# Summing the first and the last two chunks of a second product tile by tile, where two token tiles take over the accumulation banks of two others

## The chip, the cores and the metric

The kernel runs on one core of one Trainium2 chip. That core has TensorE (PE, the matrix unit), VectorE (DVE), ScalarE (ACT), GpSimd (POOL) and SyncE (SP, which here only starts transfers). Each engine works through its own queue of instructions in order; semaphores tie the queues together. The metric is the time of one execution of the whole program in device microseconds (us), as a median over runs. Matrix products leave their results in eight PSUM banks of 128 partitions by 512 fp32 values.

## What the kernel must compute

The reference is an attention layer with a decay, followed by a feed-forward layer over the same tokens (B = 8 batches, H = 8 heads, S = 576 positions, 64 values per head: 4608 tokens of 512 values; w_in is 512 x 2048, w_out 2048 x 512):

```python
scores = scale * q @ k^T
decay  = cum[:, None] - cum[None, :]        # cum = cumsum(log(clip(f)))
scores = where(causal, -1e9, scores + decay)
attn   = softmax(scores) @ v                # per batch and head
x      = attn, as 4608 tokens x 512
h      = x @ w_in                           # first product, 4608 x 2048
g      = max(h, 0) + log1p(exp(-abs(h)))
out    = g @ w_out                          # second product, 4608 x 512
```

All of it is fp32. The kernel reaches that accuracy on PE by splitting each operand in a high and a low part and adding three products of parts: high x high, high x low and low x high.

## The kernel before, in words

**Blocks, chunks, tiles.** The feed-forward part goes through the tokens in ten blocks: two of 256 tokens, then eight of 512. The 2048 columns of `h` are cut into 16 chunks of 128. For one wide block (512 tokens) the first product fills one bank `h` per chunk (`up_part`, L989, 12 matmuls at L1023), ACT and DVE turn it into `g` and its parts `gh` and `gl` (`gate`, L1050), and the second product adds chunk after chunk into the accumulators: a block has four output tiles of 128 tokens, each needs one bank (`acc_0` to `acc_3`), and every chunk adds three matmuls of 512 columns into each (`products`, L1103, the matmul at L1108: `gh` with the high part of w_out, `gh` with its low part, `gl` with its high part).

**Two passes and the switch.** The banks are shared with attention: four have the tag `att`, two `h`, and only two `acc`. So blocks 2 to 7 sum two tiles at a time (`ahead = 2`). In the first pass `down_part` (L1117) adds each chunk into `acc_0` and `acc_1` as the chunks are made, and `keep` (L1080) stores the half of `gh` and `gl` that belongs to tiles 2 and 3 to DRAM (`g_d`). After chunk 15 `finish` (L1185) copies each accumulator to a buffer `ob` (the copy is recorded at L209, on ACT or DVE) and stores it to `out` (L1195). The second pass, `second` (L1152), loads the stored parts back, two chunks in a load (`gh_0b`, `gl_0b` hold chunks 0 and 1, up to `gh_7b`), and adds them into `acc_2` and `acc_3`, which take the same two banks. This place, where the last chunks go into `acc_0` and `acc_1` and the first into `acc_2` and `acc_3`, is called a switch below; there are six, one for each of blocks 2 to 7. The last two blocks get two banks from attention, which is over by then, and have no switch.

**Order.** Nothing of the order is written out by hand. Every piece of work is added to a list with what it needs and which banks or buffers it takes (`tags`); a planner (`Plan`, L46) gives each engine its queue by list scheduling: of the next 700 pieces it takes again and again the one that by its table of costs can start first, the earlier added one where two tie. Feed-forward pieces are added between those of attention by a budget of time (`run_ffn`). `add_block` (L1229) lines up a block's pieces: the second product of a chunk runs `LAG` = 2 chunks behind its first product, and the last six pieces of a block's second pass are held back and put between the first chunks of the next block, where no second product is at hand yet.

**Attention** runs through the same queues: q and k come as `raw` (L653), are split and moved into `T` (L209, a cast on ACT or DVE, and L692), scores `s` (L736, L737), their row minima `negm` (L741, DVE), the weights `p` (L761, an exponential on ACT), the row sums (L773, L774), `p` times the reciprocal `rsum` (L783 on ACT, L785 on POOL), the transposes of `p` into `b` (L815), their parts `ph` (L209) and `pl` (L830), the product with v, `o` (L863, L869), and the shift of `o` into the rows `x` of the feed-forward part (L887 on ACT, L896 on DVE). Transposed names such as `s_1` count the rows' tiles in one head.

Of the kernel before, what the change touches and what calls it, by code (L numbers as in the profile page):

```python
# [212 lines left out]
def tile_decay_attention_softplus_ffn(  # L213
# [19 lines left out]
    NT, DM = out.shape  # L233
# [706 lines left out]
    def ffn_block(i):  # L940
# [175 lines left out]

        def down_part(u, k):  # L1117
            box, ready, kept = st["g", u]
            fc = u * nk + k
            tags = (("acc", "acc") + late_banks)[:ahead]  # L1120

            def mm(e):
                if fc == 0:
                    begin(range(ahead), tags)
                if plain:
                    for tt in range(ntile):
                        e.matmul(  # L1127
                            st["acc", tt], box["g"][:, (2 * k + tt) * P : (2 * k + tt + 1) * P],
                            w_out32[fc], start=fc == 0, stop=fc == NFC - 1,
                        )  # L1130
                    return
                products(e, fc, range(ahead), *(box[x][:, k * nt :] for x in "hl"))

            op = add(
                on_pe32(DM * ahead) if plain else on_pe(DM, 3 * ahead), mm,
                after=ready + ([w_out_ready[fc]] if plain else w_out_done[fc]) + st["downs"][-1:],
                takes=tags if fc == 0 else (),
            )
            st["downs"].append(op)
            if plain:  # L1140
                w_out_read[fc] = [op]
                splits_left.extend([lambda: split_w_in(fc), lambda: split_w_out(fc)])
            if k == nk - 1:
                give("gh", [op])
                if not plain:
                    give("gl", [op] + kept)
                if kept:

                    plan.gives[op][-2][1][0] += 1
                    plan.gives.setdefault(kept[0], []).append(plan.gives[op][-2])  # L1150

        def second(fp, k):  # L1152

# [10 lines left out]
            def mm(e):  # L1164
                if fc == 0:
                    begin(range(ahead, ntile), ("acc",) * 2)
                products(
                    e, fc, range(ahead, ntile), *(st[x, fp][:, k * TB :] for x in ("gh", "gl"))
                )

            if k == 0:
                need = [st["kept", fc], st["kept", fc + 1]]
# [3 lines left out]
            op = add(  # L1176
                on_pe(DM, 3 * (ntile - ahead)), mm, after=[st["second", fp]] + st["downs"][-1:],
                takes=("acc",) * 2 if fc == 0 else (),
            )
            st["downs"].append(op)  # L1180
            if k:
                give("gh", [op])
# [25 lines left out]
        for u in range(NFC // nk):  # L1208
# [6 lines left out]
            downs.append([(down_t, lambda u=u, k=k: down_part(u, k)) for k in range(nk)])  # L1215
        downs[-1].append((0.0, lambda: finish(range(ahead))))
        tail = []
        if ahead < ntile:
            tail = [
                (down_t, lambda fp=fp, k=k: second(fp, k)) for fp in range(NFP) for k in range(2)  # L1220
            ] + [(0.0, lambda: finish(range(ahead, ntile)))]
        return [(0.0, split_x)], ups, downs, tail
# [6 lines left out]
    def add_block(i):  # L1229
        head, ups, downs, tail = ffn_block(i)  # L1230

        n = min(6, kept_units[0], len(ffn)) if ffn and not late else 0
        last = [ffn.pop() for _ in range(n)][::-1]
        ffn.extend(head)
        for u, d in zip(ups, downs):
            ffn.extend(u)
            late.append(d)
            if last:
                ffn.extend(last[:2] if len(late) <= LAG else last)
                last = last[2:] if len(late) <= LAG else []  # L1240
            if len(late) > LAG:
# [149 lines left out]
```

## Time and profile before

| what | value |
|---|---|
| median of three runs | 1230.14 us (1228.51, 1230.14, 1230.23) |
| the profiled execution | 1233.55 us, of which its span is 1231.4 us and 2.15 us lie around it |
| PE busy | 1209.8 us of the span (98%) in 6512 matmuls |
| DVE, ACT, POOL busy | 868.2 us (70%), 863.5 us (70%), 140.4 us (11%) |
| granted clock of PE | mean 0.993 of full speed |
| transfers | 168.40 MB, a mean of 137 GB/s over the span |
| matmuls of the two-pass second product (L1108) | 3 x 352 as the page groups them, some 0.39 to 0.41 us each from start to modelled end |
| first matmul of acc_2 at the six switches | at 368.10, 498.37, 629.10, 762.94, 896.81 and 1027.38 us of the span |

Matmuls overlap, so that the time from one start to the next is what a matmul costs, not its own duration. A row of the timeline gives start, duration, engine, line, operation, output and inputs; what stands in brackets at its end is the time that the engine had waited for the piece named there. Rows of ACT and DVE overlap slightly too, by an instruction's tail.

### The profile page before, as it was taken

The page shows a single profiled execution, that of the slowest core. Times are in us where ns is not written, and L with a number is a line of the kernel's source. Part 1 is how long each engine was busy: PE and PEld are TensorE (multiplying, and loading weights), DVE is VectorE, ACT ScalarE, POOL GpSimd, SP SyncE. Part 2 cuts the span into 40 slices and gives each one's busy share as a digit, 9 for nine tenths or more (in the row PEclk, how much of TensorE's full clock was granted, in tenths as well). Part 3 has the DMA queues.
Part 4 walks back from the last instruction along what each step waited for, and adds up shares of the span by engine and source line. Part 5 has one row for each costly group of instructions (what it writes and reads, how often), then busy time and mean ns, then how long its engine had stood idle before and what let it go on. Part 6 is the DMA issues. An engine that isn't in the chain of part 4 may idle for free.

```text
span 1231.4 us, 19804 instructions
## 1 busy us (share of the span) xinstructions
PE 1209.8 (98%) x6512; PEld 1007.8 (82%) x6512; DVE 868.2 (70%) x2138; ACT 863.5 (70%) x2055; POOL 140.4 (11%) x121
## 2 busy tenths in 40 slices
PE   7899999999999999999999999999999999999998
PEld 5676688888888888888888888888888888888887
DVE  6988889998787778767786778577866774223322
ACT  4576688888787777777787787687867874444543
POOL 3621012011011000010001000100011000000000
PEclk9799999999999999999999999999999999999999
DMA  7865435335455454654474446453565435211210
GB/s 214 259 179 146 133 93 152 112 91 177 121 173 174 130 151 138 186 168 120 122 220 133 138 126 186 129 165 108 149 174 169 122 95 160 80 52 52 86 52 35
DMA packets 100199, 168.40 MB, mean 137 GB/s; under 512 B 10496, under 2 KB 74008, under 8 KB 100096
## 3 DMA queue, kind: packets, MB, share of 16 engines
q1 hardware_dynamic: 100096, 167.13, 46.0%
q8 instruction: 52, 0.85, 0.3%
q14 instruction: 51, 0.42, 0.1%
HBM read 127.85 MB, written 39.24 MB: 136 GB/s over the span
## 4 chain that ended last, share of the span: by engine, by line
PE 82%; DVE 7%; ACT 5%; DMA 3%; issue 2%; POOL 1%; SPq 0%; DVEq 0%; POOLq 0%; ACTq 0%
PE h L1023 28%; PE acc L1108 27%; PE b L815 7%; PE o L869 6%; PE s L737 3%; PE s L736 3%; DMA raw<-in_qkT 2%; PE h L1004 2%; PE s L734 2%; ACT p L761 2%; PE fill L1299 2%; PE o L863 1%; PE acc L1127 1%; DVE s L741 1%; ACT p L783 1%
## 5 line engine op out<-in xcount | busy, mean ns | idle before, releaser
L1023 PE MATMUL h<-xh,wih 128*128 128x512 f32 (+1 forms) x576 | 230.5, 403 | 0.6 <-DVE gl L1078 0.6
L761 ACT ACTIVATE p<-s,negm 128x288 f32<-128x288 f32 (+7 forms) x384 | 183.1, 480 | 51.7 <-DVE negm L741 49.1
L1023 PE MATMUL h<-xl,wih 128*128 128x512 f32 (+1 forms) x576 | 216.8, 379 | 0.0
L1070 DVE SCALAR_TENSOR_TENSOR h<-h,e 128x512 f32<-128x512 f32 x136 | 95.1, 699 | 136.8 <-ACT e L1062 135.0
L741 DVE CUSTOM_DVE_ANT_0 s<-s,cmask 128x288 f32<-128x288 f32 (+5 forms) x320 | 137.4, 437 | 63.1 <-PE s L737 53.4
L785 POOL TENSOR_SCALAR p<-p,rsum 128x448 f32<-128x448 f32 (+3 forms) x72 | 91.3, 1273 | 788.5 <-DVE rsum L774 436.9
L1056 ACT ACTIVATE e<-h 128x512 f32<-128x512 f32 x144 | 85.7, 595 | 117.5 <-PE h L1023 115.9
L830 DVE TENSOR_TENSOR pl<-b,ph 128x512 fp32r<-128x512 f32 (+1 forms) x224 | 126.1, 569 | 49.3 <-ACT ph L209 48.2
L1023 PE MATMUL h<-xh,wl 128*128 128x512 f32 (+1 forms) x576 | 148.6, 380 | 0.0
L815 PE MATMUL b<-ident,p 128*128 128x128 f32 x960 | 145.7, 275 | 1.1 <-POOL p L785 0.3
L1108 PE MATMUL acc<-woh_dt_float32r,gh 128*128 128x512 f32 x352 | 143.4, 407 | 0.0
L1108 PE MATMUL acc<-woh_dt_float32r,gl 128*128 128x512 f32 x352 | 137.8, 392 | 0.0
L1108 PE MATMUL acc<-wol_dt_float32r,gh 128*128 128x512 f32 x352 | 137.2, 390 | 0.0
L815 PEld LDWEIGHTS b<-ident,p 128*128 128x128 f32 x960 | 114.1, 140 | 24.0 <-issue 3.2
L1023 PEld LDWEIGHTS h<-xh,wih 128*128 128x128 f32 x576 | 108.8, 189 | 16.9 <-DVE gl L1078 0.8
L1023 PEld LDWEIGHTS h<-xh,wl 128*128 128x128 f32 x576 | 104.8, 188 | 21.4
L1023 PEld LDWEIGHTS h<-xl,wih 128*128 128x128 f32 x576 | 108.8, 189 | 14.4
L783 ACT ACTIVATE p<-p,rsum 128x192 f32<-128x192 f32 (+6 forms) x227 | 106.7, 536 | 18.2 <-DVE rsum L774 17.5
L209 ACT CAST ph<-b 128x512 fp32r<-128x512 f32 (+1 forms) x150 | 81.7, 546 | 52.2 <-PE b L815 50.9
L1078 DVE TENSOR_TENSOR gl<-h,gh 128x512 fp32r<-128x512 f32 x136 | 93.5, 687 | 27.5 <-ACT gh L209 26.2
L869 PE MATMUL o<-ph,vhl 128*128 128x320 f32 x448 | 105.2, 264 | 0.0
L736 PE MATMUL s<-T 128*64 128x64 f32 x336 | 99.6, 306 | 4.0 <-ACT p L761 2.9
(156 smaller groups left out, 2382.0 us busy)
## 6 DMA issues: line engine op xcount, KB each, us to landing
wl<-wil_d SPq DMA_DIRECT2D x72, 512.0 KB
raw<-in_qkT SPq DMA_DIRECT2D x112, 288.0 KB
g_d<-gh SPq DMA_DIRECT2D x96, 128.0 KB
g_d<-gl SPq DMA_DIRECT2D x96, 128.0 KB
vr<-in_vR SPq DMA_DIRECT2D x64, 160.0 KB
out<-ob SPq DMA_DIRECT2D x36, 256.0 KB
sto<-in_w_out SPq DMA_DIRECT2D x11, 512.0 KB
sti<-in_w_in SPq DMA_DIRECT2D x9, 512.0 KB
```

The source lines that it names most:

```text
L736: e.matmul(o, qA[:, q0:end], kA[:, a:z], start=True, stop=False)
L741: e.tensor_tensor_reduce(out=box["o"], in0=box["o"], in1=cmask[0:n_q, right - w : right], scale=-0.125, scalar=m0 if i else 3.0e38, op0=AL ...
L761: e.activation(o, box["o"], AF.Exp, bias=m1, scale=-1.0, accum_out=acc)
L783: e.activation(a, a, AF.Copy, scale=f_)
L785: e.tensor_scalar(a, a, f_, None, ALU.mult)
L815: e.transpose(box["ps"][:, at : at + P], pt[pi][:, c : c + P], ident)
L830: e.tensor_sub(box["l"], box["ps"][:, pad : pad + w], box["h"].bitcast(F32))
L869: e.matmul(box["ps"][:, a - g0 : z - g0], st["vhl"][:, vc, :], pbox[x][:, o : o + z - a], start=i == 0 and m == 0, stop=i == len(todo) - 1 ...
L1023: e.matmul(o, l, r, start=m == 0, stop=m == 11)
L1070: e.scalar_tensor_tensor(h, h, 0.0, box["e"], ALU.max, ALU.add)
L1078: e.tensor_sub(box["l"], box["t"], box["h"].bitcast(F32))
L1108: e.matmul(st["acc", tt], l, r[fc], start=fc == 0 and m == 0, stop=fc == NFC - 1 and m == 2,)
```

## The change

The second product's pieces can now hold one tile instead of two. `down_part` and `second` take a list of tiles. In blocks 2 to 7 the last two chunks of the first pass (14 and 15) are no longer added chunk by chunk into both accumulators: `acc_0` gets chunk 14 and chunk 15, is finished (copied and stored), and only then `acc_1` gets its chunks 14 and 15 and is finished. In the second pass the first load (chunks 0 and 1) and the last (chunks 14 and 15) are treated in the same way: both chunks into `acc_2`, then both into `acc_3`, with a `finish` after each tile in the last. A bank is asked for tile by tile too: `acc_2` takes one bank, `acc_3` the other when its first piece comes. The buffers `gh` and `gl` of chunk 14 are given back only after the last tile's piece, and `gh` and `gl` of chunk 15 likewise. `add_block` holds back nine pieces of the second pass instead of six; the last pieces are now half as long, and two, three and the rest of them go between the next block's chunks.

```diff
--- before.py
+++ after.py
@@ -1114,14 +1114,14 @@
             for tt, tag in zip(tiles, tags):
                 st["acc", tt] = bank(tag, f"acc{i}_{tt}")
 
-        def down_part(u, k):
+        def down_part(u, k, tiles=range(ahead)):
             box, ready, kept = st["g", u]
             fc = u * nk + k
-            tags = (("acc", "acc") + late_banks)[:ahead]
+            tags = [(("acc", "acc") + late_banks)[tt] for tt in tiles]
 
             def mm(e):
                 if fc == 0:
-                    begin(range(ahead), tags)
+                    begin(tiles, tags)
                 if plain:
                     for tt in range(ntile):
                         e.matmul(
@@ -1129,10 +1129,11 @@
                             w_out32[fc], start=fc == 0, stop=fc == NFC - 1,
                         )
                     return
-                products(e, fc, range(ahead), *(box[x][:, k * nt :] for x in "hl"))
+                o = k * nt + tiles[0] * P
+                products(e, fc, tiles, *(box[x][:, o:] for x in "hl"))
 
             op = add(
-                on_pe32(DM * ahead) if plain else on_pe(DM, 3 * ahead), mm,
+                on_pe32(DM * ahead) if plain else on_pe(DM, 3 * len(tiles)), mm,
                 after=ready + ([w_out_ready[fc]] if plain else w_out_done[fc]) + st["downs"][-1:],
                 takes=tags if fc == 0 else (),
             )
@@ -1140,7 +1141,8 @@
             if plain:
                 w_out_read[fc] = [op]
                 splits_left.extend([lambda: split_w_in(fc), lambda: split_w_out(fc)])
-            if k == nk - 1:
+            if k == nk - 1 and tiles[-1] == ahead - 1:
+
                 give("gh", [op])
                 if not plain:
                     give("gl", [op] + kept)
@@ -1149,7 +1151,7 @@
                     plan.gives[op][-2][1][0] += 1
                     plan.gives.setdefault(kept[0], []).append(plan.gives[op][-2])
 
-        def second(fp, k):
+        def second(fp, k, tiles=range(ahead, ntile)):
 
             fc = 2 * fp + k
 
@@ -1163,22 +1165,21 @@
 
             def mm(e):
                 if fc == 0:
-                    begin(range(ahead, ntile), ("acc",) * 2)
-                products(
-                    e, fc, range(ahead, ntile), *(st[x, fp][:, k * TB :] for x in ("gh", "gl"))
-                )
-
-            if k == 0:
+                    begin(tiles, ("acc",) * 2)
+                o = k * TB + (tiles[0] - ahead) * P
+                products(e, fc, tiles, *(st[x, fp][:, o:] for x in ("gh", "gl")))
+
+            if ("second", fp) not in st:
                 need = [st["kept", fc], st["kept", fc + 1]]
                 d = st["second", fp] = add_dma(load, 512, 2, after=need, takes=("gh", "gl"))
                 for c in (fc, fc + 1):
                     kept_read[c] = [d]
             op = add(
-                on_pe(DM, 3 * (ntile - ahead)), mm, after=[st["second", fp]] + st["downs"][-1:],
-                takes=("acc",) * 2 if fc == 0 else (),
+                on_pe(DM, 3 * len(tiles)), mm, after=[st["second", fp]] + st["downs"][-1:],
+                takes=("acc",) * len(tiles) if fc == 0 else (),
             )
             st["downs"].append(op)
-            if k:
+            if k and tiles[-1] == ntile - 1:
                 give("gh", [op])
                 give("gl", [op])
 
@@ -1213,12 +1214,29 @@
             ]
             ups.append(parts + [(0.0, lambda u=u: gate(u))])
             downs.append([(down_t, lambda u=u, k=k: down_part(u, k)) for k in range(nk)])
-        downs[-1].append((0.0, lambda: finish(range(ahead))))
         tail = []
         if ahead < ntile:
-            tail = [
-                (down_t, lambda fp=fp, k=k: second(fp, k)) for fp in range(NFP) for k in range(2)
-            ] + [(0.0, lambda: finish(range(ahead, ntile)))]
+
+
+            downs[-2:] = [[], []]
+            for tt in range(ahead):
+                downs[-1] += [
+                    (down_t / 2, lambda u=u, tt=tt: down_part(u, 0, [tt]))
+                    for u in (NFC - 2, NFC - 1)
+                ] + [(0.0, lambda tt=tt: finish([tt]))]
+            for fp in range(NFP):
+                if fp in (0, NFP - 1):
+                    for tt in range(ahead, ntile):
+                        tail += [
+                            (down_t / 2, lambda fp=fp, k=k, tt=tt: second(fp, k, [tt]))
+                            for k in range(2)
+                        ]
+                        if fp:
+                            tail.append((0.0, lambda tt=tt: finish([tt])))
+                else:
+                    tail += [(down_t, lambda fp=fp, k=k: second(fp, k)) for k in range(2)]
+        else:
+            downs[-1].append((0.0, lambda: finish(range(ahead))))
         return [(0.0, split_x)], ups, downs, tail
 
 
@@ -1229,15 +1247,16 @@
     def add_block(i):
         head, ups, downs, tail = ffn_block(i)
 
-        n = min(6, kept_units[0], len(ffn)) if ffn and not late else 0
+        n = min(9, kept_units[0], len(ffn)) if ffn and not late else 0
         last = [ffn.pop() for _ in range(n)][::-1]
         ffn.extend(head)
         for u, d in zip(ups, downs):
             ffn.extend(u)
             late.append(d)
             if last:
-                ffn.extend(last[:2] if len(late) <= LAG else last)
-                last = last[2:] if len(late) <= LAG else []
+                m = 1 + len(late) if len(late) <= LAG else len(last)
+                ffn.extend(last[:m])
+                last = last[m:]
             if len(late) > LAG:
                 ffn.extend(late.pop(0))
         if tail:
```

The number of matmuls, copies, casts and transfers is the same. Both versions' queues are the same, apart from the numbers in the names, outside some 20 us round each switch and the last load of each second pass. How pieces move on the queues is seen at three places. In the rows, `acc_1` is the second tile of the first pass, `acc_2` and `acc_3` are those of the second; `gh_0b` and `gl_0b` are the first load of the second pass.

**PE at the second switch** (block 3). Before:

```order
L869 MATMUL o_1_5628<-ph_3_5605,vhl_5056 128x64
L869 MATMUL o_1_5628<-pl_3_5610,vhl_5056 128x64
L736 MATMUL s_0_0_5661<-T_1172 64x64
L737 MATMUL s_0_0_5661<-T_1172 64x64
L736 MATMUL s_1_0_5664<-T_1172 128x192
L737 MATMUL s_1_0_5664<-T_1172 128x192
L1108 MATMUL acc_2_5671<-woh_dt_float32r,gh_0b 128x512
```

Now:

```order
L1108 MATMUL acc_1_4728<-woh_dt_float32r,gl_15_5622 128x512
L736 MATMUL s_1_0_5664<-T_1172 128x192
L737 MATMUL s_1_0_5664<-T_1172 128x192
L736 MATMUL s_2_0_5669<-T_1172 128x320
L737 MATMUL s_2_0_5669<-T_1172 128x320
L736 MATMUL s_3_0_5677<-T_1172 128x448
L737 MATMUL s_3_0_5677<-T_1172 128x448
L815 MATMUL b_0_5692<-ident,p_128_95 128x128
L815 MATMUL b_0_5692<-ident,p_256_96 128x128 x2
L815 MATMUL b_0_5692<-ident,p_384_97 128x128 x2
L1108 MATMUL acc_2_5700<-woh_dt_float32r,gh_0b 128x512
```

The scores `s_2` and `s_3` and the first transposes `b_0` of a head now stand ahead of `acc_2`'s first matmul; before, only `s_0` and `s_1` did. At the third switch the change brings the same order.

**PE at the fourth switch** (block 5). Before:

```order
L869 MATMUL o_1_8692<-pl_3_8690,vhl_8128 128x64
L736 MATMUL s_1_0_8731<-T_1172 128x192
L737 MATMUL s_1_0_8731<-T_1172 128x192
L736 MATMUL s_2_0_8738<-T_1172 128x320
L737 MATMUL s_2_0_8738<-T_1172 128x320
L736 MATMUL s_3_0_8750<-T_1172 128x448
L737 MATMUL s_3_0_8750<-T_1172 128x448
L815 MATMUL b_0_8763<-ident,p_128_95 128x128
L815 MATMUL b_0_8763<-ident,p_256_96 128x128 x2
L815 MATMUL b_0_8763<-ident,p_384_97 128x128 x2
L1108 MATMUL acc_2_8771<-woh_dt_float32r,gh_0b 128x512
```

Now:

```order
L1108 MATMUL acc_1_7800<-woh_dt_float32r,gl_15_8699 128x512
L1108 MATMUL acc_2_8742<-woh_dt_float32r,gh_0b 128x512
L1108 MATMUL acc_2_8742<-wol_dt_float32r,gh_0b 128x512
L1108 MATMUL acc_2_8742<-woh_dt_float32r,gl_0b 128x512
L1108 MATMUL acc_2_8742<-woh_dt_float32r,gh_0b 128x512
L1108 MATMUL acc_2_8742<-wol_dt_float32r,gh_0b 128x512
L1108 MATMUL acc_2_8742<-woh_dt_float32r,gl_0b 128x512
L1108 MATMUL acc_3_8761<-woh_dt_float32r,gh_0b 128x512
L1108 MATMUL acc_3_8761<-wol_dt_float32r,gh_0b 128x512
L1108 MATMUL acc_3_8761<-woh_dt_float32r,gl_0b 128x512
L736 MATMUL s_1_0_8767<-T_1172 128x192
L737 MATMUL s_1_0_8767<-T_1172 128x192
```

Here `acc_2` follows `acc_1`'s last matmul at once, and the scores and transposes that stood ahead of it come after six matmuls into `acc_2` and three into `acc_3`. The first and the fifth switch have much the same order now (`acc_2` six times in a row, scores between or behind).

**SP at the fourth switch** (the queue of transfer starts). Before:

```order
L1159 DMA gh_0b<-g_d 128x2x256
L1159 DMA gl_0b<-g_d 128x2x256
L1195 DMA out<-ob_0_8734 128x512
L1195 DMA out<-ob_1_8736 128x512
L1159 DMA gh_1b<-g_d 128x2x256
L1159 DMA gl_1b<-g_d 128x2x256
L1159 DMA gh_2b<-g_d 128x2x256
L1159 DMA gl_2b<-g_d 128x2x256
L653 DMA raw_8798<-in_qkT 64x1152 x2
```

Now:

```order
L1161 DMA gh_0b<-g_d 128x2x256
L1161 DMA gl_0b<-g_d 128x2x256
L1082 DMA g_d<-gh_15_8688 128x256
L1082 DMA g_d<-gl_15_8699 128x256
L1161 DMA gh_1b<-g_d 128x2x256
L1161 DMA gl_1b<-g_d 128x2x256
L1196 DMA out<-ob_0_8724 128x512
L1196 DMA out<-ob_1_8749 128x512
L653 DMA raw_8770<-in_qkT 64x1152 x2
L1161 DMA gh_2b<-g_d 128x2x256
L1161 DMA gl_2b<-g_d 128x2x256
```

The two loads `raw` of the next head now stand ahead of `gh_2b` and `gl_2b`. The change also puts them ahead of `gh_2b` at the first switch and behind `gl_2b` at the third and fifth, each the other way round before; at the second they stay behind.

## The prediction, made before the changed kernel was timed

> **What bounds the kernel now.** I read the page first. PE is busy for nearly the whole span, at nearly full clock:
>
> ```profile
> span 1231.4 us, 19804 instructions
> PE 1209.8 (98%) x6512; PEld 1007.8 (82%) x6512; DVE 868.2 (70%) x2138; ACT 863.5 (70%) x2055; POOL 140.4 (11%) x121
> ```
>
> The change removes no matmul, so only PE's waits can change: at most 21.6 us in the whole span, and of those only the ones that lie where the order changes. The view of PE's waits names the wait on a bank that is to be taken over:
>
> ```profile
> PE acc L1108 <- ACT ob L209: 0.9, 2, 0.7
> ```
>
> 0.9 us in two waits, one of 0.73 us at the sixth switch. That is all that the tile-by-tile order can win directly. But at the other switches the planner has put scores and transposes of attention where PE would wait for the bank, and these have waits of their own. I therefore cut out, at each switch, the same 111 PE instructions: from the first matmul of chunk 14 into acc_0 to the end of the second of the two `gh_2b`/`gl_2b` chunks (at the sixth, with little attention left, a shorter piece of 10 us). The view of windows gives their length, then the busy times, the granted clock, the DMA share and GB/s:
>
> ```profile
> 362.89:381.89 19.00, 18.80 (x115) 16.47 (x113) 16.44 (x48) 15.25 (x41) 3.67 (x3) 1.00 0.78 241
> 493.21:512.16 18.95, 18.80 (x114) 16.52 (x112) 16.14 (x47) 15.69 (x41) 1.20 (x2) 1.00 0.76 222
> 623.43:643.44 20.01, 19.82 (x114) 16.54 (x113) 15.97 (x44) 16.74 (x43) 1.94 (x2) 1.00 0.73 220
> 754.57:777.61 23.04, 20.20 (x115) 16.50 (x113) 18.58 (x51) 16.62 (x45) 2.49 (x2) 1.00 0.69 199
> 888.70:910.85 22.15, 21.49 (x115) 17.55 (x114) 17.19 (x49) 17.04 (x47) 3.54 (x3) 0.92 0.66 197
> ```
>
> The same work takes 18.95 us at best. Above that the five switches lose 0.05, 0, 1.06, 4.09 and 3.20 us, the sixth its 0.9: some 9.3 us in all. These losses are what the change plays for, in both directions.
>
> **Where the fourth switch loses 4.09.** PE's timeline there, before and after the first matmul of acc_2 (762.94):
>
> ```profile
> 759.56 0.36 PE L736 MATMUL s<-T 128*128 128x192 f32 x1
> ...
> 760.30 0.31 PE L737 MATMUL s<-T 68*128 68x320 f32 x1
> 761.34 0.47 PE L736 MATMUL s<-T 128*128 128x448 f32 x1 [0.73 <-ACT p L761]
> ...
> 762.14 1.04 PE L815 MATMUL b<-ident,p 128*128 128x128 f32 x5
> 762.94 0.48 PE L1108 MATMUL acc<-woh_dt_float32r,gh_0b 128*128 128x512 f32 x1
> ...
> 771.94 0.40 PE L1108 MATMUL acc<-woh_dt_float32r,gl_1b 128*128 128x512 f32 x1
> 774.21 0.36 PE L736 MATMUL s<-T 128*128 128x192 f32 x1 [1.88 <-ACT p L761]
> ```
>
> A matmul of 512 columns costs 0.227 us from start to start, by a row of the chain of waits (start, time, number):
>
> ```profile
> 1219.02 8.17 PE acc L1108 x36
> ```
>
> So the second loss is plain: 771.94 to 774.21 is 2.27 us, of which 2.04 are lost. The first is the rest, 4.09 - 2.04 = 2.05 us: s_3 waits for a bank that the weights `p` of s_0 free, and b_0 for its scaled `p`. ACT's timeline shows why both are late:
>
> ```profile
> 759.79 0.20 ACT L761 ACTIVATION_READ_ACCUMULATOR p<-s,negm 128x1 f32 x1
> 759.88 0.58 ACT L209 COPY ob<-acc 128x512 f32<-128x512 f32 x1
> 760.49 0.37 ACT L887 COPY x<-o 64x256 f32<-64x256 f32 x1
> 760.89 0.31 ACT L761 ACTIVATE p<-s,negm 64x64 f32<-64x64 f32 x1
> ...
> 761.44 1.92 ACT L783 ACTIVATE p<-p,rsum 64x64 f32<-64x64 f32 x4 [0.15 <-DVE rsum L774]
> ...
> 771.85 1.82 ACT L209 CAST T<-raw 128x576 fp32r<-128x576 f32 x3 [3.48 <-DMA raw<-in_qkT]
> ```
>
> In its queue the copy of acc_1 and the shift of `o` stand ahead of the small `p`, and the scalings behind that. Later the cast of `raw` holds ACT for 3.48 us. `raw` was started on SP's queue behind two stores and four loads of the second pass:
>
> ```profile
> 760.59 0.83 SPq L1195 DMA_DIRECT2D out<-ob  x2
> ...
> 763.19 0.41 SPq L1159 DMA_DIRECT2D gl_2b<-g_d  x1
> 763.70 1.11 SPq L653 DMA_DIRECT2D raw<-in_qkT  x2
> ```
>
> That is 8.15 us from start to cast.
>
> **The change, switch by switch.** Matmuls, copies and transfers keep their number and sizes; splitting a chunk's piece in two adds no instruction. So each term is the loss after less the loss before, with the order on each queue as the rows above the prediction show it.
>
> First switch: acc_2's six matmuls follow acc_1's directly, 6 x 0.227 = 1.36 us of work that covers the copy of acc_1 (0.58 us); the copy of acc_0 is covered by acc_1's. Nothing is left to win or lose: -0.05 (0 to its 0.05 lost, and at worst 1.1, as at the fourth below).
>
> Fourth switch: the same cover. The 2.05 us in front of acc_2 go, since scores and transposes now come behind nine matmuls. What is late next is the copy of acc_1, which ACT reaches behind the small `p`, the shift and a cast of v: 759.99 (end of the accumulator's read) + 0.31 + 0.37 + 0.46 + 0.58 = 761.71. The 0.46 is this cast elsewhere:
>
> ```profile
> 906.17 0.46 ACT L209 CAST vhl<-vr 128x320 fp32r<-128x320 f32 x1
> ```
>
> PE, which is through all that stood ahead of s_1 at 759.56, would be through acc_2's six matmuls at 760.92. That leaves a wait of 0.79. Bounds: 0, if DVE frees the ACT queue earlier, and 1.1, with one more `p` of 0.31 in front. `raw` stands ahead of `gh_2b` now, as at the third switch, which lost 1.06 at most, so the 2.04 go as well. Loss after 0.8, term -3.29.
>
> Second and third switch: both get nearly the order that the fourth had: s_1, s_2, s_3 and b_0 ahead of acc_2, `raw` behind `gl_2b`. I price them by it: 2.05 each in front of acc_2. Against full weight speaks that the small `p` now stands ahead of the shift and of the copy; for it, that the scalings which b_0 needs come behind shift, cast of v and copy, 1.41 us together. With `p` ending at 760.30 the scalings would start at 761.71, no earlier than the 761.44 of the row above. So I take 2.05; the bounds are 0 and 2.05. For the hold by `raw`, 2.04 at most and nothing at least (at the second switch `raw` already stood behind `gl_2b` and no wait came of it): at the second six more matmuls on `gh_2b` stand ahead of the scores, 1.36, so 0.68; at the third none, and I take 0.5, nearer to the second switch's row than to the fourth's. Terms: +2.73 (0 + 2.05 + 0.68) and 2.05 + 0.5 - 1.06 = +1.49.
>
> Fifth switch: 3.20 lost before. Its clock was 0.92 over 22.15 us, which is 1.77 us; the other 1.43 are waits like these:
>
> ```profile
> 894.84 0.47 PE L736 MATMUL s<-T 128*128 128x448 f32 x1 [0.31 <-DVE x L896]
> 895.84 1.32 PE L815 MATMUL b<-ident,p 128*128 128x128 f32 x5 [0.33 <-POOL p L785]
> 896.81 0.78 PE L1108 MATMUL acc<-woh_dt_float32r,gh_0b 128*128 128x512 f32 x1
> ```
>
> Now s_1 and s_2 come first, then acc_2's six. The copy of acc_1 stands behind three scalings on ACT (four take 1.92 us above, so some 1.4); a cast of `T` stands ahead of the cast of chunk 15 (one of three: 1.82 / 3 = 0.6). Against these 2.0 us stand the same 1.36 us of cover and 0.69 of three more matmuls, which would hide them; but `raw` goes behind `gl_2b` here, up to 2.04. With nothing to choose between them I take the middle of the bounds, a loss of 1.9 between 0 and 3.8 (2.04 and 1.77 of clock): term -1.3.
>
> Sixth switch: acc_1's six matmuls cover the copy of acc_0, and acc_2's six that of acc_1. The 0.9 go; chunk 15's `gl` is wanted 0.68 us earlier (three matmuls), which may cost up to that, and I take 0.4: term -0.5 (-0.9 to -0.2).
>
> The rest: nine held-back pieces are the same work as six (six of them halves, three whole); outside the switches the queues agree. 0.
>
> Sum: -0.05 + 2.73 + 1.49 - 3.29 - 1.3 - 0.5 = -0.92 us. The profiled execution took 1231.4 + 2.15 = 1233.55 us, 3.41 above the median of 1230.14; the change by the same difference gives 1232.6 for a profiled execution and **1229.2 us** for the median.
>
> On the clock, the fifth switch shows a fall to 0.92 over its stretch with no PE wait longer than 0.33 us in the rows, and the fourth none with one of 1.88 us. The Trainium skill (TensorE: Matmul & The Clock Gate, Why this matters for your kernels) says that the clock falls after gaps in PE's work of more than about 3 us. The trace does not agree: none here is that long. By the rule no stretch after the change would have a dip; by the rows one may come or stay anywhere, 1.77 us each.
>
> **The rivals.**
>
> *Faster, the cover works everywhere.* The small `p` ahead of the copy lets s_3 start on time at the second and third switch, b_0 finds its scalings done, `raw` is in time as it was at the second switch, and no dip comes. Then these two lose at most 0.5 each and the fifth 0.5 (the terms +0.5, -0.56, -2.7), with -0.05, -3.29 and -0.5: -6.6, 1223.5 us. For it: the first two switches ran without a wait with s_0 and s_1 in front of acc_2. Against: more is in front now, and ACT's queue is no shorter. With all losses gone it would be 1230.1 - 9.3 = 1220.8, the lower bound.
>
> *Slower, ACT is late at three switches.* One mechanism: `raw` behind `gl_2b` holds ACT's queue at its cast, as in the row of 3.48 us, and the scores behind it wait. In full at the second, third and fifth switch it costs 0.68, 2.04 and 2.04, with the 2.05 in front of acc_2 at the first two. Terms: +2.73, 2.05 + 2.04 - 1.06 = +3.03, 2.04 + 1.77 - 3.20 = +0.61 with the dip, -3.29, -0.05, -0.2: +2.8, 1233 us; a second dip makes it 1234.7. It decides from a hold of about 1.5 us at both of the latter two. For it: the fourth switch. Against: the first and second had the same order of `raw` and PE didn't wait.
>
> *No change but the bank's wait.* PE's queue shifts its waits about, the total stays, and only the 0.9 go: 1230.14 - 0.9 = 1229.2 us, the forecast's time by another way. For it: the loss differs from switch to switch without any difference in the work. Against: the fourth's -3.29 is well grounded in the rows.
>
> **How the numbers follow.** A measurement here tells about 0.2% (2.46 us) from no change. The forecast holds 0.36, the case of the bank's wait alone 0.14, the faster 0.28, the slower 0.22. A fifth of the forecast's share lies beyond -2.46 (the terms at the second and third switch are the softest, 2.05 each): faster 0.28 + 0.07 = 0.35; slower 0.17 of the slower rival's share and 0.04 of the forecast's: 0.21; the rest, 0.44, the same. The forecast's own range is 1226.5 to 1232; the range that holds 8 in 10 reaches to both rivals: 1223.0 to 1233.5.
>
> **What would show it.** Right: at the fourth and fifth switch the 111 instructions shrink to about 19.8 and 20.8 us, at the second and third they grow to about 21.7 and 21.5, and in PE's waits the bank's 0.9 is gone. The rows in front of acc_2 at the second switch then show s_3 or b_0 waiting for `p`. Wrong on the faster side: these two stay within 0.5 us of 18.95. Wrong on the slower side: a cast of `T` on ACT that waits for `raw` at two of the switches, or a clock below 1.00 in a stretch where none is now. Wrong altogether: waits outside the stretches, since the orders agree there.

## The result and the profile after

The change made the kernel slower: 1238.47 us in the median of six runs (1236.89 to 1241.79) against 1230.38 (1228.51 to 1232.37), a ratio of 1.0071 with a 95% interval of 1.0057 to 1.0084. The profiled execution took 1241.35 us with a span of 1239.6 us. Its page begins:

```profile
span 1239.6 us, 19789 instructions
PE 1212.1 (98%) x6512; PEld 1007.9 (81%) x6512; DVE 869.1 (70%) x2137; ACT 863.2 (70%) x2054; POOL 142.1 (11%) x123
```

The matmuls are as many as before, and the busy times of ACT, DVE and the weight loads are the same within 1 us. Of the 8.2 us by which the span grew, 2.3 are busy time of PE (1209.8 us before), which ran longer at half clock, and the other 5.9 are its waits. In the view of PE's waits (total, number, longest) these two rows grew most. Before:

```profile
PE s L736 <- ACT p L761: 2.9, 3, 1.9
...
PE s L736 <- DVE x L896: 0.3, 1, 0.3
```

After:

```profile
PE s L736 <- ACT p L761: 5.3, 4, 2.4
...
PE s L736 <- DVE x L896: 2.5, 1, 2.5
```

The row for the copied bank (`acc` <- ACT `ob`, 0.9 us before) is gone from this view: the waits that the change was made for did go. In their place stand waits of attention's scores. The view of windows, for the same 111 PE instructions at the first five switches:

```profile
361.52:381.08 19.56, 19.05 (x114) 16.46 (x113) 16.30 (x48) 16.35 (x41) 3.45 (x3) 1.00 0.84 260
492.31:515.27 22.96, 19.91 (x115) 16.33 (x113) 16.12 (x44) 16.77 (x44) 2.30 (x3) 1.00 0.64 184
626.68:649.59 22.91, 19.99 (x115) 16.28 (x113) 16.85 (x45) 16.58 (x44) 3.26 (x3) 1.00 0.75 199
761.22:781.60 20.38, 19.30 (x114) 16.49 (x113) 17.93 (x50) 15.95 (x40) 3.10 (x3) 1.00 0.81 243
893.11:918.53 25.42, 22.21 (x114) 18.59 (x113) 17.80 (x49) 18.65 (x49) 2.85 (x2) 0.87 0.71 195
```

Against before (19.00, 18.95, 20.01, 23.04, 22.15) that is +0.56, +4.01, +2.90, -2.66 and +3.27 us, +8.08 in all, and the spans differ by 8.2. So the loss lies round the switches. (Outside them small differences cancel: -1.4 us ahead of the first, some +0.5 ahead of the fourth and the fifth and +0.35 at the end. They were not followed further.)

At the second switch PE's timeline shows one long wait:

```profile
498.52 0.33 PE L815 MATMUL b<-ident,p 128*128 128x128 f32 x1 [0.28 <-POOL p L785]
499.00 0.89 PE L815 MATMUL b<-ident,p 128*128 128x128 f32 x4 [0.16 <-ACT p L783]
...
510.03 0.39 PE L1108 MATMUL acc<-woh_dt_float32r,gl_2b 128*128 128x512 f32 x1
512.96 0.35 PE L736 MATMUL s<-T 128*128 128x192 f32 x1 [2.55 <-DVE x L896]
```

From 510.03 to 512.96 are 2.93 us where a matmul needs 0.23: 2.70 lost. In front of acc_2 the two waits for scaled `p` are short. ACT's timeline with one row of DVE's, and under it SP's, tell why:

```profile
505.10 1.05 ACT L209 CAST xh<-x 128x1024 fp32r<-128x1024 f32 x1
510.25 1.82 ACT L209 CAST T<-raw 128x576 fp32r<-128x576 f32 x3 [4.09 <-DMA raw<-in_qkT]
512.09 0.37 ACT L887 COPY x<-o 64x256 f32<-64x256 f32 x1
```

```profile
512.49 0.42 DVE L896 TENSOR_TENSOR x<-o,x 64x256 f32<-64x256 f32 x1 [3.69 <-ACT x L887]
```

```profile
495.34 0.43 SPq L1161 DMA_DIRECT2D gh_0b<-g_d  x1
...
496.58 2.39 SPq L1196 DMA_DIRECT2D out<-ob  x2
499.06 0.39 SPq L1161 DMA_DIRECT2D gh_1b<-g_d  x1
...
500.60 0.42 SPq L1161 DMA_DIRECT2D gl_2b<-g_d  x1
501.11 1.11 SPq L653 DMA_DIRECT2D raw<-in_qkT  x2
```

`raw` starts at 501.11 and its cast at 510.25, 9.14 us later; ACT stands for 4.09 us with the shift of `o` (L887) queued behind the cast. DVE adds that shift to `x` (L896), and only then has `s_1` its bank: the row's "DVE x" is the last link of a chain that begins at `raw`. Ahead of `raw` stand, within 6 us, six loads of the second pass of 256 KB each and two stores of as much. Before the change `raw` had stood behind the same six loads here, but the first four of them had started earlier, `gh_0b` 9.0 and `gh_1b` 6.4 us ahead of `raw` instead of 5.8 and 2.1:

```profile
491.99 0.37 SPq L1159 DMA_DIRECT2D gh_0b<-g_d  x1
...
494.63 0.36 SPq L1159 DMA_DIRECT2D gh_1b<-g_d  x1
...
501.01 2.33 SPq L653 DMA_DIRECT2D raw<-in_qkT  x2
```

```profile
507.73 1.24 ACT L209 CAST T<-raw 128x576 fp32r<-128x576 f32 x2
```

The cast came 6.72 us after `raw`'s start then, and ACT waited for nothing. At the third and the fifth switch, where the change puts `raw` behind `gl_2b`, it is as at the second: the cast waits 4.45 and 2.58 us, `s_1` 2.28 and 2.44.

```profile
644.40 1.24 ACT L209 CAST T<-raw 128x576 fp32r<-128x576 f32 x2 [4.45 <-DMA raw<-in_qkT]
...
909.97 1.82 ACT L209 CAST T<-raw 128x576 fp32r<-128x576 f32 x3 [2.58 <-PE s L737]
```

The last row names a score of PE and not `raw`. The chain of waits of the same execution has the transfer of `raw` from 902.96 to 909.87, so `raw` landed 0.1 us ahead of this cast; in the repeat below the same row names `raw`.

### The profile page after: what moved, and what is told of

The parts are those of the page before. It is cut to its first block, busy times and chain, and to the rows that moved or that the text cites. A ratio compares the mean times of both kernels' runs of the same rounds, so it can differ in the third digit from the quotient of the medians.

```text
span 1239.6 us, 19789 instructions
## 1 busy us (share of the span) xinstructions
PE 1212.1 (98%) x6512; PEld 1007.9 (81%) x6512; DVE 869.1 (70%) x2137; ACT 863.2 (70%) x2054; POOL 142.1 (11%) x123
## 4 chain that ended last, share of the span: by engine, by line
PE 74%; DVE 9%; ACT 7%; DMA 7%; issue 2%; SPq 1%; POOL 0%; DVEq 0%; ACTq 0%; POOLq 0%
PE h L1023 26%; PE acc L1108 24%; PE b L815 6%; PE o L869 5%; DMA raw<-in_qkT 3%; PE s L736 2%; PE s L737 2%; PE h L1004 2%; ACT p L761 2%; PE acc L1127 2%; PE o L863 2%; PE s L734 1%; DVE s L741 1%; DMA xh_st<-in_w_in 1%; ACT p L783 1%
## 5 line engine op out<-in xcount | busy, mean ns | idle before, releaser
L785 POOL TENSOR_SCALAR p<-p,rsum 128x448 f32<-128x448 f32 (+3 forms) x74 | 94.1, 1278 | 794.1 <-DVE rsum L774 404.5
```

The source lines that it names most:

```text
L785: e.tensor_scalar(a, a, f_, None, ALU.mult)
```

## The experiments

All times below are medians; a ratio is against the kernel before, timed on the same chip beside the variant. Line numbers shift by a few in kernels with added code. **Theory A** is that `raw` lands late because of what is queued ahead of it on SP's queue, and holds ACT. **Theory B** is that it is late for its single buffer, so that its place on the queue hardly matters. **Theory C** adds to A that the loads ahead bunch up because chunk 14's buffers come free later.

**raw ahead of the third pair's loads at three switches.** The loads `gh_2b`, `gl_2b` are held until `raw` has been started:

```diff
+                if i in (3, 4, 6) and fp in (2,):
+                    held.append(start)      # start() issues the two loads
+                else:
+                    start()
 ...
                 st["raw"] = raw[:, 0, :], raw[:, 1, :]
+                while held:
+                    held.pop(0)()
```

> The changed kernel with one thing moved on SP's queue at the second, third and fifth switch: the two loads raw of the next head stand ahead of gh_2b and gl_2b instead of behind them. All other orders are the same. Theory A (raw lands late because the 512 KB of gh_2b and gl_2b, bunched with gh_1b and the two stores, go through the DMA engines first): raw's way from start to cast falls from 9.1, 9.0 and 7.6 us to below 7, PE's wait at s_1 falls from 2.55, 2.28 and 2.44 us to below 0.6 each, and the median falls by 5 to 8 us, to 1230.5 to 1233.5. Theory B (raw lands late because its single buffer comes free late, at DVE's last subtraction from it, and its place on the queue hardly matters): the three waits stay above 1.5 us and the median stays above 1236.

1229.83 us (1227.37 to 1232.64), ratio 0.9997 (0.9986 to 1.0008): 8.6 us less than the changed kernel (6.1 less than in its repeat below), by two rows moved on one queue at three places. The windows of the second, third and fifth switch:

```profile
492.08:513.29 21.21, 19.96 (x114) 16.24 (x113) 16.13 (x44) 16.80 (x44) 2.30 (x3) 1.00 0.67 199
624.69:645.07 20.38, 19.74 (x115) 16.35 (x114) 16.64 (x45) 16.65 (x44) 3.19 (x3) 1.00 0.73 216
888.20:908.68 20.48, 19.41 (x115) 16.46 (x113) 17.16 (x49) 17.03 (x43) 2.85 (x2) 1.00 0.78 231
```

They shrink by 1.75, 2.53 and 4.94 us; of the last some 2.8 us are the clock, which didn't fall here (6.20 us from `s_1` to the stretch's end before, 3.37 now). At the second, `raw` is started at 500.31 instead of 501.11, and the cast begins 7.95 us after that instead of 9.14:

```profile
500.31 1.12 SPq L654 DMA_DIRECT2D raw<-in_qkT  x2
501.52 0.54 SPq L1167 DMA_DIRECT2D gh_2b<-g_d  x1
```

```profile
508.26 1.82 ACT L209 CAST T<-raw 128x576 fp32r<-128x576 f32 x3 [2.31 <-DMA raw<-in_qkT]
```

The waits at `s_1` are 0.72 us, none and 0.28. The expectation of a way below 7 us failed at the second switch (7.95), where the wait of 0.72 is a little above "below 0.6"; the median fell 0.6 us more than expected. The third and the fifth switch are the clean cases: `raw` starts no earlier in the stretch than in the changed kernel (8.72 and 9.18 us from its begin, 8.70 and 9.26 there), the two loads start 2.7 and 2.2 us later, and the cast comes 5.76 and 5.56 us after `raw`'s start instead of 9.02 and 7.60. So what stands ahead of `raw` sets when it lands. Theory B, which wanted waits above 1.5 and a median above 1236, is out, though its buffer does set when `raw` can start: at the third switch of the changed kernel it starts at 635.38, right behind DVE's last subtraction from that buffer (634.69 to 635.37). The Trainium skill (DMA: Bandwidth & Descriptors, Rules for kernel authors) says of two transfers to disjoint halves of the partitions that they serialize: issued by one engine, both go through the same ring on each of the DMA engines. This run shows the like for a load behind other loads: with the 512 KB behind it, `raw` was cast 2.0 to 3.3 us sooner after its start at these two switches.

**raw behind them at the other two switches**, the opposite move: at the first and the fourth, where the change has `raw` ahead.

```diff
+                if fp == 1 and i in (2, 5):
+                    armed.append(1)         # raw's start is held from here
+                elif fp == 2:
+                    armed.clear()
+                    while held:
+                        held.pop(0)()       # after gh_2b, gl_2b
```

> The changed kernel with raw put behind gh_2b and gl_2b at the first and the fourth switch too, where the change has it ahead of them; nothing else is moved. Theory A (the bytes queued ahead of raw set its landing): PE's wait at s_1 there grows from 0.30 us and nothing to 1.5 to 2.5 us each, the two stretches from 19.56 and 20.38 to 21 to 23 us, and the median by 3 to 5 us against the changed kernel, to 1241 to 1243.5. Theory B: no change, 1238.5.

1241.53 us (ratio 1.0106, 1.0073 to 1.0138), against 1235.94 for the changed kernel on the same chip: +5.6. The two stretches:

```profile
361.68:384.71 23.03, 20.62 (x115) 17.65 (x113) 17.73 (x49) 17.91 (x46) 3.95 (x3) 0.93 0.78 233
761.63:783.36 21.73, 19.51 (x114) 16.57 (x113) 18.14 (x50) 16.27 (x40) 3.30 (x3) 1.00 0.81 232
```

`s_1` waits 2.18 us at the first and 1.14 at the fourth, where the expectation said 1.5 to 2.5; the first also ran part of its time at half clock. The waits come where `raw` is put behind the loads, as A said. The size is less sure: against the changed kernel's first measurement the median is only 3.1 us more, and the two intervals overlap.

**The changed kernel again**, for a second profile beside these.

> The changed kernel once more, beside the other variants: 1238.5 us, PE's three waits at s_1 of 2.3 to 2.6 us at the second, third and fifth switch. If the fall of the clock at the fifth switch (6.8 us long) belongs to the wait there, it comes again at one of the three; if it comes by chance, the stretch of the fifth is 22.3 us without it.

1235.94 us (ratio 1.0059, 1.0037 to 1.0081). Its five stretches took 19.10, 22.40, 21.42, 20.39 and 23.32 us, with waits at `s_1` of 1.94, 0.77 and 1.57 at the second, third and fifth, less than the 2.3 to 2.6 expected: `raw`'s way differs from run to run, and the median is 2.5 us below that of the first measurement. The change's loss is 5 to 8 us by these two medians. The clock fell again, at the fifth, for half as long:

```profile
888.22:911.54 23.32, 20.98 (x114) 17.64 (x113) 17.80 (x49) 18.55 (x49) 2.86 (x2) 0.93 0.72 212
```

**The same move in the kernel before**, at the fourth switch (block 5), the only one at which it lost time to `raw`; the diff is the first one's with `i in (5,)`.

> The kernel before with raw ahead of gh_2b and gl_2b at the fourth switch, the only one that loses time to raw there. Theory A: PE's wait of 1.88 us behind ACT's cast goes to below 0.5, the fourth switch's 111 instructions take about 21.1 us instead of 23.04, the median falls by 1.5 to 2 us (ratio 0.9985). Theory B: the stretch stays at 23 us, ratio 1.000.

1228.65 us, ratio 0.9985 (0.9974 to 0.9996), as A said. The wait of 1.88 us at `s_1` is gone from PE's timeline. The stretch took 22.66 us, not 21.1: in this execution the clock was down there (0.92 over 22.66 us, 1.8 us) and not at the fifth, which took 20.54.

**Which half of the change makes it.** First the first pass alone tile by tile:

```diff
-                if fp in (0, NFP - 1):
+                if fp in ():
...             # finish both at once, six pieces held back, as before
```

> The changed kernel with the first pass alone tile by tile (chunks 14 and 15 into acc_0, then acc_1); both accumulators of the second pass are summed together as before. PE's queue in front of acc_2 at the second and third switch is the changed kernel's, and raw stands behind gl_2b at all five switches. If the first pass's half makes the loss: the second and third stretch take 22.5 to 23.5 us, the first, fourth and fifth lose 1.5 to 2.5 us to raw too, the median is 1237 to 1242. If the second pass's half does it: below 1233.

1239.31 us (ratio 1.0083, 1.0056 to 1.0110). PE waited for the first score behind `raw`'s cast at all five switches, 1.11 to 1.62 us each (1.5 to 2.5 was expected at the first, fourth and fifth); the second stretch took 23.01 us with a fall of the clock (0.95), the third 21.85, under what was expected. So the first pass's half is enough for a loss of this size, by `raw` at five switches instead of three. Then the second pass's first load alone, chunks 14 and 15 as before:

```diff
-            downs[-2:] = [[], []]
-            for tt in range(ahead): ...
+            downs[-1].append((0.0, lambda: finish(range(ahead))))
...
-                if fp in (0, NFP - 1):
+                if fp in (0,):
...             # finish both at once, six pieces held back, as before
```

> The kernel before with the second pass's first load alone tile by tile (chunks 0 and 1 into acc_2, then into acc_3), chunks 14 and 15 of both passes as before. SP's queue keeps its order of raw and the loads at all switches. If the first pass's half makes the loss: each stretch within 0.6 us of the kernel before (a fall of the clock apart), the median 1229 to 1231.5. If the second pass's half does it: above 1233.

1233.46 us (ratio 1.0025, 1.0012 to 1.0038): more than expected, although its one profiled execution, 1229.52 us, showed no stretch longer than before by more than 1 us. So it was profiled once more, and once with `raw` moved ahead at the first, second and fourth switch.

> The same kernel without that move, for a second profile: the first profiled execution was 1229.52 us, 3.9 below the median of its runs, with stretches within 1 us of the kernel before. If raw's landing makes the loss, one of the first four stretches has a longer wait at s_1 here, 1 to 2 us more than in the first profile.

> The kernel with the second pass's first load alone tile by tile, and raw ahead of gh_2b at the first, second and fourth switch. If its loss of 2.6 us against the kernel before is raw's late landing as well (ACT waited for it 0.85, 0.78 and 3.27 us at these three), the waits go and the median falls from 1233.5 to 1228 to 1229.5. If something else makes it, the median stays above 1231.

Again it took 1233.85 us, and its first stretch showed what the first profile had missed: a wait of 1.66 us at `s_1` behind the cast, 0.95 more than in that profile, with half clock after it. (At the fourth the wait was 1.09 us, less than the 1.66 of the first profile.)

```profile
360.10:382.52 22.42, 20.57 (x115) 17.73 (x112) 17.88 (x49) 17.52 (x45) 4.45 (x4) 0.92 0.84 238
```

With `raw` moved it took 1228.85 us (ratio 0.9984, 0.9970 to 0.9999), 5.0 less, the first stretch 19.01. The same move at the fourth switch had won 1.7 us in the kernel before as well; the other 3.3 are as much as the second half had lost. So its loss is `raw`'s landing too.

**Are chunk 14's buffers the reason that the loads bunch?** Two runs. In the first only chunk 15 is added tile by tile, chunk 14 into both accumulators as before:

```diff
-            downs[-2:] = [[], []]
+            downs[-1:] = [[]]
...
-                    (down_t / 2, lambda u=u, tt=tt: down_part(u, 0, [tt]))
-                    for u in (NFC - 2, NFC - 1)
+                    (down_t / 2, lambda tt=tt: down_part(NFC - 1, 0, [tt]))
```

> The changed kernel with chunk 14 added into both accumulators at once as before, and only chunk 15 tile by tile. Theory C (the loads of the second pass bunch up ahead of raw because chunk 14's buffers are held until acc_1's piece of chunk 14 is done, six matmuls later): gh_0b and gh_1b start 6 and 3 us ahead of acc_2 again at the first three switches, the second and third stretch take at most 20.5 us instead of 22.96 and 22.91, ACT's wait for raw there stays below 2.5 us, and the median comes out near 1231 to 1233 (the fourth switch has raw behind gl_2b here and may lose up to 2 us more than in the changed kernel). Rival (the order of scores and tiles round acc_2 does it, not the buffers): the second and third stretch stay above 22 us.

1231.86 us (ratio 1.0009, 0.9998 to 1.0019). `gh_0b` and `gh_1b` start 5.8 and 3.1 us ahead of acc_2 again at the second switch, and the first three stretches took 18.76, 19.82 and 19.41 us without a wait of ACT for `raw`. At the fourth, where `raw` stands behind `gl_2b` and the loads start late, it lost as much as anywhere:

```profile
750.69:775.87 25.18, 21.36 (x114) 17.68 (x113) 18.15 (x51) 17.60 (x46) 3.03 (x2) 0.93 0.73 199
```

In the second run the kernel before only counts chunk 14's buffers as free later:

```diff
+            if ahead < ntile and u == NFC - 2:
+                st["late14"] = kept
-            if k == nk - 1:
+            elif k == nk - 1:
...             # gives back both chunks' buffers here
```

> The kernel before, with chunk 14's buffers counted as free only when chunk 15 has been added, and nothing else: PE, ACT, DVE and POOL keep their orders word for word; on SP's queue the loads gh_1b and gl_1b at the first, second, third and sixth switch slip behind the store of chunk 15 (and two small loads of T's rows ahead of it). Theory C (late buffers alone bunch the loads ahead of raw): gh_1b starts about 1.5 to 2 us later against acc_2, raw's way at the first two switches grows from 5.5 to 6.5 us by 0.5 to 1.5 us, ACT waits for it up to 2 us there, PE loses 0.3 to 1.5 us at each, the third switch (raw ahead of gh_2b) loses nothing, and the median is 1230.5 to 1233. Rival (the order of the scores and tiles): no row moves by more than 0.3 us, the median stays within 1 us of the kernel before.

1231.35 us (ratio 1.0003, 0.9993 to 1.0013). The second stretch lost 1.4 us (20.39, a wait of 0.87 at `s_1`), the first nothing; the fourth took 24.99 us with a wait of 2.26 and a fall of the clock (0.93). The median lies in the expectation of C and in its rival's; the rival's other half, that no row moves by more than 0.3 us, did not hold, but `s_1` also waited 0.66 us behind `raw` at the second switch in the run above whose queues are there the kernel's before. So late buffers of chunk 14 alone cost about nothing that can be measured. With the order of PE also changed, as in the first of the two, they may count; the two were not separated further.

**Versions that gain.** The change in block 5 alone, where it had won (the lists of tiles are made for `i in (5,)` only):

> The kernel before with the whole change made in block 5 alone (the fourth switch and the last load of that block); its queues are the kernel's before at all other switches. If the switches are independent of each other, the fourth stretch takes 20.4 us instead of 23.04, as in the changed kernel, the others stay as before, and the median falls by 2.0 to 2.7 us (ratio 0.998). If a switch's loss is handed on to the next blocks, the others move and the gain is below 1 us.

1227.79 us, ratio 0.9976 (0.9967 to 0.9985). The fourth stretch took 20.38 us as in the changed kernel, the first three 19.00, 18.95 and 20.00 as before: a switch neither hands its loss on nor takes over another's. And chunk 15 alone tile by tile, with `raw` ahead at the third, fourth and fifth switch:

> The kernel with only chunk 15 tile by tile, with raw ahead of gh_2b at the third, fourth and fifth switch (at the fourth the small load vr goes along with it). Theory A: PE's wait of 3.55 us at the fourth falls below 1.2, its stretch from 25.18 to 20 to 22 us, the fifth to 20.5 to 21 without a fall of the clock, and the median from 1231.86 to 1226.5 to 1229, so that it would stand beside the change made in block 5 alone (1227.79). Theory B (queue place irrelevant): no change against 1231.86.

1227.82 us, ratio 0.9983 (0.9971 to 0.9996). Its fourth stretch:

```profile
752.64:773.54 20.90, 19.98 (x115) 16.42 (x114) 17.69 (x51) 16.13 (x40) 2.59 (x2) 1.00 0.83 244
```

25.18 us became 20.90, with a wait of 0.65 at `s_1` where there had been 3.55. Both versions beat the kernel before and the changed one.

## Why the prediction was wrong

The forecast was 1229.2 us, no change that can be measured, in a range of 1223.0 to 1233.5. The measured 1238.47 lies outside, above the slower rival's 1234.7 too. Switch by switch, in us:

| switch | forecast | profile | second profile |
|---|---|---|---|
| first | -0.05 | +0.56 | +0.10 |
| second | +2.73 | +4.01 | +3.45 |
| third | +1.49 | +2.90 | +1.41 |
| fourth | -3.29 | -2.66 | -2.65 |
| fifth | -1.3 | +3.27 | +1.17 |
| sixth | -0.5 | +0.15 | -0.09 |
| sum | -0.92 | +8.23 | +3.39 |

(The sixth is the stretch of 201 PE instructions from chunk 14 on: 41.87 us before, 42.02 and 41.78. The second profile is that of the repeated run, 1235.00 us, below its median.)

The step that failed is the **hold by `raw`**, the term set at 0.68 us for the second switch, 0.5 for the third and a share of 1.9 for the fifth. It measured 2.70, 2.44 (a wait of 2.28) and 2.6 us (a wait of 2.44). Moving `raw` on the queue took the whole loss away, from 1.0071 to 0.9997 of the time before, the falls of the clock behind these waits included. The mechanism and its place were seen, and stood as the slower rival with a chance of 0.22. Two choices kept it small. At the second switch 1.36 us of matmuls were set against it, as if `raw` would land when it did at the fourth; but `raw` took longer, 9.14 us to its cast instead of 8.15, and ate that cover. At the third, 0.5 was taken because `raw` behind `gl_2b` had cost nothing at the second switch before. That row was the wrong one to lean on: there the first two pairs of loads (`gh_0b`, `gh_1b`) had started 6.4 and 3.7 us ahead of acc_2, and after the change they start 4.3 and 0.6 us ahead at this switch, together with the stores. The order of the queue was compared, and not the times at which its rows would start. Why the loads bunch so stays open after the two runs on chunk 14's buffers.

**In front of acc_2** at the second and third switch, 2.05 us each was forecast. The stretches leave 1.3 and 1.5 us (4.01 - 2.70 and 3.96 - 2.44) for this and all the rest: too high by a third. This part of the loss is not `raw`'s: with `raw` ahead, 1.5 us stay at the second (2.26 less the 0.72 at `s_1`) and 1.4 at the third. The small `p`, now ahead of the shift, came in time for `s_3`, as the faster rival had it, and b_0 waited some 0.4 us for its scalings, as the forecast had it.

**The fourth switch** did what was forecast, -2.66 and -2.65 for -3.29. The loss of 1.4 us that stays is not the copy of acc_1 (forecast 0.8), which no row waits for. It is mostly `o` and a small score ahead of the switch, which wait for `x` and `pl`; that part of the term came near by luck:

```profile
763.24 0.39 PE L869 MATMUL o<-ph,vhl 128*128 128x256 f32 x1 [0.54 <-DVE x L896]
...
764.52 0.21 PE L736 MATMUL s<-T 128*64 128x64 f32 x1 [0.55 <-DVE pl L830]
```

**The fifth** was forecast to gain 1.3 with the middle of its bounds, 0 to 3.8 us of loss; it lost 6.47. Besides the hold, 2.6, the clock of 0.87 over 25.42 us is a fall worth about 3.3, part of it inside the wait; some 2.8 fell on matmuls. A second fall of 1.77 us had been in the rival's upper figure, not in the range.

**The sixth** shows a wait that takes another's place. The bank's wait went (0.73 us here; the forecast counted all 0.9, of which 0.20 stood at the first switch), and PE waits for the second pair's load, which now starts later:

```profile
1039.13 0.50 PE L1108 MATMUL acc<-woh_dt_float32r,gl_1b 128*128 128x512 f32 x1 [0.30 <-DMA gl_1b<-g_d]
```

The forecast's 0.4 us for `gl_15` was the wrong successor; nothing was gained there in either profile.

The rival in which only the bank's wait goes is out: it did go, and the time rose.

## What to carry to other kernels

A change that takes a bank's wait away wins of itself at most that wait (0.9 us here); the rest, from -2.66 to +4.01 us at a switch, comes from the order that the planner lays out anew. Look at the transfers there first: one load behind a bunch of others on the shared queue held an in-order engine for 4 us and TensorE for 2.5. To price such a load, compare when the transfers ahead of it start and how much they move, not only their order; and where a split helps at some places and hurts at others, make it only where it helps (block 5 alone: 0.9976) or move the load that is needed first to the front of the queue.

## What was not expected of the hardware

**The same transfer at the same place of the queue takes a varying time.** With `raw` behind `gl_2b` in the changed kernel's order, its cast at the second switch began 9.14 us after its start in one profile and 8.53 in the other, and the wait at the third was 2.28 and 0.77 us. Where it stood ahead of `gh_2b`, at the fourth, ACT did not wait for it in any of the three profiles of that order; at the first, also ahead, it waited 0.44 us in one of the three. So one profile of such a kernel can miss its typical loss by several us, as the first profile of the second half's variant did.

**The clock falls more often behind a wait of PE, and does not need a long one.** Over the first five switches of the fourteen profiles here, 20 stretches had a wait of 1.0 us or more at a score, and 8 of them a granted clock below 1.00; of the other 50, 3 had one. The first three switches show it by themselves (3 of 9 against none of 33), the last two less clearly (5 of 11 against 3 of 17). In the eight the clock fell between 0.7 us ahead of the start of the matmul that had waited and 1.4 us behind it, and stayed at half for 3.4 us, once for 6.8. One stretch fell with no wait longer than 0.33 us (the fifth switch of the kernel before), and one with a wait of 2.55 us didn't. The Trainium skill (TensorE: Matmul & The Clock Gate, Why this matters for your kernels) gives gaps of more than about 3 us as what to avoid. The traces do not agree with that as a threshold: in ten of the eleven stretches with a fall no wait was that long. Whether a wait causes the fall, or only makes it likelier, these runs do not tell.
